# How x is turned, and the order of the first stage, in a kernel that mixes a spectral filter and a recurrence

## The chip, the core and the metric

The kernel runs on one core of one Trainium2 chip. The metric is the device time of one launch in microseconds, the median of several runs. A core has five engines that each work through a list of instructions of their own: TensorE (PE in the profile; its weight loads are PEld), VectorE (DVE), ScalarE (ACT), GpSimd (POOL) and SyncE (SP), which here only issues DMAs. They wait for each other by semaphores. DMAs are issued from a queue of SyncE, ScalarE or GpSimd and are carried out by the core's 16 DMA engines.

## The reference

The input x has 2048 tokens of 1024 features, in bfloat16. Two branches are mixed by a gate of each token.

```
g = sigmoid(sum(x * gate_w))                     # one number a token
a = irfft2(rfft2(x) * (w_r + 1j*w_i))            # over tokens and features
Bu = x @ B_bar.T                                 # B_bar complex, 1024 x 1024
h_t = Lam_bar * h_(t-1) + Bu_t                   # over the 2048 tokens
b = 2 * real(h @ C.T) + x * Dskip
out = g * a + (1 - g) * b
```

## The kernel before

**The spectral branch.** The transform over the features (called the d-transform, or fd) and the first step of the transform over the tokens (s1) work on 16 rows of tokens. Row j holds the 128 tokens whose number is j modulo 16. For a row, `fold` (VectorE, lines 661 and 662) adds and subtracts the two halves of the features, `fd(j)` (line 332) multiplies the folded row by a table G in eight matmuls and copies the result out as X1, and `s1(j)` (line 342) multiplies X1 by a table T2 in four matmuls and copies the result out as A1. A1 is stored to a scratch in DRAM (`turn_scratch`, line 353). Later stages load it in another order (`load`, line 377), take the second token step (`s2`, line 457), multiply by the weights W, and go back by two inverse token steps (`is1`, `is2`, lines 478 to 513) and the inverse d-transform (`spectral`, line 595).

**The recurrence.** `unit(c, q)` (line 253) treats chunk c of 256 tokens (eight chunks) and half q of the 1024 states. It has two halves on TensorE (line 300): 32 matmuls of B with x for the real part, 32 for the imaginary part, each followed by a copy from PSUM on ScalarE (line 302). Chunk c takes eight tokens of each of the 16 rows' two halves, so each unit reads all 16 rows of x. After its second half the unit puts seven pieces of VectorE work on a list (line 305): a rotation by a table (`turn_back`), its sums (`join`), two scans (line 275), the carry into the next chunk, a second rotation (`turn`) and its sums (`join_on`, lines 292 and 293). `early(tb)` (line 579) is the output of token tile tb (128 tokens, half of a chunk): two times 16 matmuls with C (line 570) and four with x and Dskip (line 574). It needs both units of its chunk to be done on VectorE, and it needs all of C and the tile `xs` of x. Six buffers hold units (NHA + NHB).

**How x comes.** x is loaded by eight plain DMAs of 512 KB (`load_x`, line 194) into `xn`, a place that later holds C (tiles CT). `turn_x(j)` (line 653) turns row j by eight TensorE transposes into PSUM, and ScalarE copies them into `xQ`, the turned x that everything else reads. B, C and the tiles `xs` come turned by transposing DMAs (lines 205, 555 and 562), issued by SyncE.

**What sets the order.** The order of the instructions of TensorE, VectorE and ScalarE is that of the program text (`manual_schedule`, line 169); the order on SyncE and GpSimd is chosen when the kernel is built. `front()` (line 768) does one row by a plan of letters: T for `turn_x`, f for `fold`, F for `fd(j + 1)`, S for `s1(j)`; `order` names the loads of B and C that follow a row. The halves of units and of token tiles form one chain, `ssm` (line 756), and `halves(ssm, 1)` issues the next one. From row 8 on one half follows each row. `vector(us)` (line 311) issues VectorE pieces from the list up to a given cost; `vector_until(c)` issues all that chunk c still needs. `tables` (`make_tab`, line 208) are pieces that make the rotation tables, four for each of four groups, with sines on ScalarE, casts on GpSimd and products on VectorE (lines 230 and 235). `gate()` (line 695) computes g's sum on TensorE and turns it through DRAM by two GpSimd DMAs. `load_Wcols` (line 733) loads two columns of W by ten GpSimd DMAs, called after row 3. A1 rows 0 to 7 lie in CT[0], rows 8 to 15 in a tile of four buffers.

**PSUM.** Until row 7 the unit's PSUM tile has one buffer (`psF`), the transposes have two (`psX`), and fd and s1 share two (`psA`). After row 7 `psX` and `psF` give way to `psU` with two buffers.

Of the kernel before, what the change touches and what calls it, by code (L numbers as in the profile page):

```python
# [28 lines left out]
NHA, NHB = 4, 2  # L29

# [78 lines left out]
def kernel(  # L109
# [55 lines left out]
    xctx = ExitStack()  # L165
    psF = xctx.enter_context(tc.tile_pool(name="psF", bufs=1, space=PSUM, reuse_waits="tile"))
    psX = xctx.enter_context(tc.tile_pool(name="psX", bufs=2, space=PSUM, reuse_waits="tile"))
    pools = {"u": psF}
# [18 lines left out]
    xn = [CT[i // 4][:, 2 * (i % 4):2 * (i % 4) + 2, :] for i in range(8)]  # L187
    x_v = x.rearrange("(p j) d -> p j d", j=16)
# [5 lines left out]
    def load_x(i):  # L194
        nc.sync.dma_start(out=xn[i], in_=x_v[:, 2 * i:2 * i + 2, :])
# [57 lines left out]
    def unit(c, q):  # L253
# [42 lines left out]
        for ri in range(2):  # L296
            psu = pools["u"].tile([P, 4, TC], FP32, name="psu", tag="psu")
            for j in range(4):
                for d8 in range(8):
                    nc.tensor.matmul(psu[:, j, :], lhsT=BT[4 * q + j][:, ri, d8, :],  # L300
                                     rhs=x_t[:, d8, :, :, 8 * c:8 * (c + 1)], start=(d8 == 0), stop=(d8 == 7))
            nc.scalar.copy(out=u[:, ri].rearrange("p b (q j) -> p b q j", j=32),  # L302
                           in_=psu.rearrange("p b (j q) -> p b q j", j=32))
            if ri == 1:
                work.extend([(2.4, turn_back), (1.5, join), (2.3, lambda: scan(0)), (2.3, lambda: scan(1)),
                             (0.4, carry_on), (2.4, turn), (1.4, join_on)])
            yield 3.5
# [19 lines left out]
    def gfnet():  # L327
# [4 lines left out]
        def fd(j):  # L332
            ps = psA.tile([P, 2, K], FP32, name="ps_fd", tag="ps")
            for cls in range(2):
                for d4 in range(4):
                    nc.tensor.matmul(ps[:, cls, :], lhsT=preTs[j][:, 4 * cls + d4, :], rhs=G_sb[:, cls, d4, :],  # L336
                                     start=(d4 == 0), stop=(d4 == 3))
            X1 = gta.tile([P, 2, K], BF16, name="X1")
            (nc.vector.tensor_copy if j in (3,5,7,) else nc.scalar.copy)(out=X1.rearrange("p r (i c) -> p r i c", c=2), in_=ps.rearrange("p c (r i) -> p r i c", r=2))  # L339
            X1s[j] = X1  # L340

        def s1(j):
# [7 lines left out]
            A1 = CT[0][:, j, :].rearrange("p (g k) -> p g k", g=2) if j < 8 else A1_4[:, j % 4]  # L350
            (nc.vector.tensor_copy if j < 8 else nc.scalar.copy)(out=A1, in_=psa)  # L351
            A1s[j] = A1
            nc.sync.dma_start(out=t1_w[j], in_=A1)
            if j in (8, 12):
                keep_A1(j - 4)

        def keep_A1(j):
            if j < 8:
                nc.vector.tensor_copy(out=Acol[:, :, 0:8].rearrange("p g j -> p j g"), in_=CT[0][:, :, 0:D:K])
                return  # L360
            nc.vector.tensor_copy(out=Acol[:, :, j:j + 4].rearrange("p g j -> p j g"), in_=A1_4[:, :, :, 0])

        A1s, X1s = {}, {}
        fft["fd"], fft["s1"] = fd, s1
        yield "front"
        keep_A1(12)
# [212 lines left out]
    def early(tb):  # L579
        psy = pools["u"].tile([P, D], FP32, name="ps_y", tag="psu")  # L580
# [14 lines left out]
    def spectral(tb, scale, home, eo_home=None):  # L595
        ZT_t = fft["ZT"]
        pse = pools["u"].tile([P, 4, H], FP32, name="ps_id", tag="psu")
# [55 lines left out]
    def turn_x(j):  # L653
        pt = psX.tile([P, 8, P], BF16, name="pt")
        for i in range(8):
            nc.tensor.transpose(out=pt[:, i, :], in_=xn[j // 2][:, j % 2, P * i:P * (i + 1)], identity=ident)  # L656
        nc.scalar.copy(out=xQ[:, :, j, :].rearrange("p d (g q) -> p d g q", g=2), in_=pt.rearrange("p d (q g) -> p d g q", g=2))  # L657

# [4 lines left out]

    A1_4 = gta.tile([P, 4, 2, K], BF16, name="A1", bufs=1)
    idle = A1_4[:, 3, 0]
# [9 lines left out]
    for cls in range(2):  # L675
        nc.sync.dma_start(out=fft["G"][:, cls], in_=cG[:, cls])
    load_T2(0, 2)
    load_x(1)
    load_x(2)
    load_T2(2, 8)  # L680
    for i in range(3, 8):
        load_x(i)
    load_T2(8, 16)
    assert step() == "front"
    for j in range(2):
        turn_x(j)
        fold(j)
    keep_warm(4)
    fft["fd"](0)
    rows = iter(range(2, 16))  # L690
    folds = iter(range(2, 16))
# [38 lines left out]
    nc.gpsimd.tensor_copy(out=Wp.rearrange("p r b c -> p (r b c)"), in_=xn[7][:, 0, 0:64])  # L730
    nc.gpsimd.tensor_copy(out=Wf, in_=xn[7][:, 0, 0:2])

    def load_Wcols():
        with nc.allow_non_contiguous_dma(reason="two columns of W"):
# [17 lines left out]
    def halves(gen, n):  # L752
# [3 lines left out]
    ssm = chain(unit(0, 0), unit(0, 1), unit(1, 0), unit(1, 1), unit(2, 0), early(0), unit(2, 1), early(1), unit(3, 0), early(2), unit(3, 1), early(3), unit(4, 0), early(4), unit(4, 1), early(5), unit(5, 0), early(6), unit(5, 1), early(7), unit(6, 0), unit(6, 1), early(8), early(9))  # L756

    order = {
        **{j: [(load_B, n)] for j, n in ((2, 1), (3, 1), (4, 1), (5, 2), (6, 2), (7, 2), (8, 2), (9, 2))},
        10: [(load_B, 3), (load_small,)],  # L760
        **{j: [(load_C, j - 11)] for j in range(11, 15)},
    }
    at = [0]
    tables = iter(())

    plan = {0: "FSTfTf", 1: "TSFfT", 2: "TFfTS", 3: "TFfTS", 4: "TFfTS", 5: "TFfTS", 6: "TFfTS", 7: "TFfTS"}

    def front(pieces=0):
        j = at[0]
        at[0] += 1  # L770
        for what in plan.get(j, "fFS"):
            if what == "T":
                for r in rows:
                    turn_x(r)
                    break
            elif what == "f":
                for r in folds:
                    fold(r)
                    break
            elif what == "F":  # L780
                if j + 1 < 16:
                    fft["fd"](j + 1)
            else:
                fft["s1"](j)
        for load, *args in order.get(j, ()):
            load(*args)
        for _ in range(pieces):
            next(tables, None)

    vps = psX.tile([P, 5, 8], BF16, name="vps", tag="pt")  # L790
# [67 lines left out]
    while at[0] < 16:  # L858
        j = at[0]
        front(0 if j < 4 else 1 if j < 6 else 2 if j < 10 else 3)  # L860
        if j >= 8:
            halves(ssm, 1)
        if j >= 9:
            vector(4.2)
        if j == 10:
            gate()
        if j == 15:
            for _ in tables:
                pass
            tctx.close()  # L870
        if j == 7:
            xctx.close()
            pools["u"] = ctx.enter_context(tc.tile_pool(name="psU", bufs=2, space=PSUM, reuse_waits="tile"))
        if j == 3:
            load_Wcols()
    for q in range(4, 8):
        load_C(q)
    for v, n in (("w", 4), ("a", 1), ("z", 2), ("q", 2), ("qn", 1), ("s2", 0), ("uv", 1)):
        assert step() == v
        for i in range(n):  # L880
# [6 lines left out]
            vector(3.0)  # L887
# [82 lines left out]
```

## Time and profile before

Three runs of the kernel took 340.03, 340.09 and 340.57 us. The profile is of one more execution; it gives that execution's span, from its first to its last instruction, and no other time of it.

| | |
|---|---|
| median of the runs | 340.09 us |
| span of the profiled execution | 338.3 us, 1.8 under the median |
| PE busy | 326.3 us (96%) |
| DVE busy | 292.1 us (86%) |
| ACT busy | 167.0 us (49%) |
| POOL busy | 32.1 us (10%) |
| chain of waits that ended last | PE 71%, DVE 23%, ACT 2% |
| line 656, TensorE transposes of x | 128, 9.7 us busy |
| line 657, copies of them on ScalarE | 16, 15.6 us |
| line 300, B with x | 1024, 116.6 us |
| line 336, d-transform | 119 of 128 recorded, 29.3 us |
| line 275, scans on VectorE | 32, 72.2 us |
| line 195, x by plain DMA | 8 of 512 KB, 5.8 us from issue to landing |
| line 205, B by transposing DMA | 16 of 256 KB, 5.1 us from issue to landing |

The profile has several views. The slices cut the span into 40 equal parts of 8.46 us and give each engine's busy share in tenths. The groups list instructions of one line and shape with their number, busy time and mean length. The view in order of time lists instructions with their start and length in microseconds, and where an engine was idle before one, for how long and what ended it. A matmul's length in the records is longer than the distance to the next one, since matmuls overlap; the distance from start to start is what it costs. The issue of a DMA is a row of the queue that issues it (SPq, POOLq), and its landing is later. Busy time of the DMA engines is a mean share of the 16.

### The profile page before, as it was taken

To read this page: it belongs to the slowest core of one execution; us is meant where nothing else is said; L and a number is where in the kernel's file an instruction comes from. 1 tells how busy PE (TensorE), PEld (TensorE's weight loads), DVE (VectorE), ACT (ScalarE), POOL (GpSimd) and SP (SyncE) were. 2 spreads that over 40 slices of the span, in tenths; PEclk is the share of its full clock that TensorE was granted. 3 is DMA by queue.
4 is the path that set the end of the run, shared out by engine and by line. 5 is a ranking of instruction groups with operands and counts; after the bars stand their busy time and mean duration, and the time that the engine had idled before them with its cause. 6 is when DMAs were issued, how large, how long until landed. Compare 5 with 4: busy or idle time off the path is not lost.

```text
span 338.3 us, 6201 instructions
## 1 busy us (share of the span) xinstructions
PE 326.3 (96%) x2414; PEld 212.3 (63%) x2446; DVE 292.1 (86%) x449; ACT 167.0 (49%) x211; POOL 32.1 (10%) x64
## 2 busy tenths in 40 slices
PE   8989899999999999999999999999999999999995
PEld 3445465666847575747566575869945876565552
DVE  2679948999999999999999999999980997999951
ACT  3697597836223145656557552646632243443510
POOL 1372012210000000000000000000000011121220
PEclk9999999999999999999999999999999999999999
DMA  7999999998893047889999735947203019856695
GB/s 263 409 192 212 203 217 213 163 215 205 274 213 102 2 129 180 227 202 272 259 284 260 200 135 153 224 127 215 62 2 125 32 31 147 168 109 94 110 145 166
DMA packets 83581, 58.71 MB, mean 174 GB/s; under 512 B 54328, under 2 KB 74304, under 8 KB 83424
## 3 DMA queue, kind: packets, MB, share of 16 engines
q1 hardware_dynamic: 80304, 55.64, 65.5%
q0 software_dynamic: 3168, 2.66, 8.3%
q8 instruction: 19, 0.31, 0.4%
q14 instruction: 10, 0.08, 0.1%
q10 hardware_dynamic: 80, 0.01, 0.0%
HBM read 30.49 MB, written 17.83 MB: 143 GB/s over the span
## 4 chain that ended last, share of the span: by engine, by line
PE 71%; DVE 23%; ACT 2%; issue 2%; DVEq 0%; ACTq 0%
PE ps_y L570 26%; PE psu L300 22%; PE ps_h L570 4%; DVE h L275 4%; PE ps_id L601 4%; PE ps_is L484 2%; PE ps_fd L336 2%; PE ps_is L509 2%; PE ps_is L485 2%; DVE CT L351 2%; PE ps_y L574 2%; PE ps_s L460 2%; DVE h L263 1%; DVE su L262 1%; DVE h L287 1%
## 5 line engine op out<-in xcount | busy, mean ns | idle before, releaser
L300 PE MATMUL psu<-xQ,BT 128*128 128x256 bf16 x1024 | 116.6, 273 | 0.8 <-ACT ye L588 0.5
L300 PEld LDWEIGHTS <-BT 128*128 128x128 bf16 x1024 | 98.8, 98 | 17.5 <-issue 4.5
L570 PE MATMUL ps_y<-CT,h 128*128 128x512 bf16 x436 | 99.5, 379 | 0.6
L570 PEld LDWEIGHTS <-h 128*128 128x128 bf16 x512 | 49.7, 98 | 55.2
L275 DVE TENSOR_TENSOR_SCAN h<-rz,h 128x1024 bf16<-128x1024 f32 x32 | 72.2, 2280 | 0.3
L302 ACT CAST h<-psu 128x1024 bf16<-128x1024 f32 x32 | 32.3, 1011 | 51.4 <-PE psu L300 51.3
L616 POOL DMA_DIRECT2D BT<-y_scratch x10 | 11.9, 1194 | 239.6 <-DVE BT L610 232.0
L588 ACT ACTIVATE ye<-ps_y,omg 128x512 f32<-128x512 f32 x20 | 12.7, 684 | 44.0 <-PE ps_y L574 28.7
L336 PE MATMUL ps_fd<-G_sb,preT 128*128 128x512 bf16 x119 | 29.3, 379 | 2.1 <-ACT X L339 1.0
L262 DVE TENSOR_TENSOR su<-h,tab 128x2048 bf16<-128x2048 bf16 x16 | 19.6, 1223 | 2.8 <-ACT h L302 2.2
L336 PEld LDWEIGHTS <-preT 128*128 128x128 bf16 x128 | 12.0, 97 | 15.4 <-issue 2.8
L287 DVE TENSOR_TENSOR h<-h,tab 128x2048 bf16<-128x2048 bf16 x16 | 20.7, 1295 | 0.5
L462 ACT CAST X<-ps_s 128x1024 bf16<-128x1024 f32 x16 | 16.2, 1014 | 8.7 <-PE ps_s L460 8.7
L263 DVE TENSOR_TENSOR h<-h,tab 128x2048 bf16<-128x2048 bf16 x16 | 19.6, 1225 | 0.8
L286 DVE TENSOR_TENSOR sg<-h,tab 128x2048 bf16<-128x2048 bf16 x16 | 19.5, 1220 | 0.1
L657 ACT COPY xQ<-pt 128x1024 bf16<-128x1024 bf16 x16 | 15.6, 1017 | 2.8 <-PE pt L656 2.7
L511 ACT CAST ZT<-ps_is 128x1024 bf16<-128x1024 f32 x16 | 15.5, 1024 | 2.2 <-PE ps_is L509 2.2
L339 ACT CAST X<-ps_fd 128x1024 bf16<-128x1024 f32 x13 | 13.2, 1012 | 6.2 <-PE ps_fd L336 6.1
L487 ACT CAST C<-ps_is 128x1024 bf16<-128x1024 f32 x16 | 16.1, 1007 | 0.0
L601 PE MATMUL ps_id<-raw,ZT 128*128 128x256 bf16 x128 | 15.9, 273 | 0.0
L570 PE MATMUL ps_h<-CT,h 128*128 128x512 bf16 x62 | 14.4, 379 | 0.1
L601 PEld LDWEIGHTS <-ZT 128*128 128x128 bf16 x128 | 12.4, 98 | 2.2
(186 smaller groups left out, 362.3 us busy)
## 6 DMA issues: line engine op xcount, KB each, us to landing
y_scratch<-ye SPq DMA_DIRECT2D x20, 256.0 KB, 2.6
CT<-in_A_x_dram SPq DMA_DIRECT2D x8, 512.0 KB, 5.8
Bb<-turn_scratch SPq DMA_DIRECT2D x16, 256.0 KB, 4.0
turn_scratch<-C SPq DMA_DIRECT2D x16, 256.0 KB, 3.7
raw<-turn_scratch SPq DMA_DIRECT2D x16, 256.0 KB, 4.2
Wb<-in_A_w_r_dram SPq DMA_DIRECT2D x32, 127.8 KB, 4.2
Wb<-in_A_w_i_dram SPq DMA_DIRECT2D x32, 127.8 KB, 4.1
out_dram<-BT SPq DMA_DIRECT2D x14, 256.0 KB, 2.5
```

The source lines that it names most:

```text
L262: nc.vector.tensor_mul(out=su, in0=u[:, ::-1], in1=bc(1))
L263: nc.vector.tensor_mul(out=u, in0=u, in1=bc(0))
L275: nc.vector.tensor_tensor_scan(out=seg, data0=rz[:, js].rearrange("p j t -> p (j t)"), data1=seg, initial=0.0, op0=ALU.mult, op1=ALU.add)
L286: nc.vector.tensor_mul(out=sg, in0=u[:, ::-1], in1=bc(3))
L287: nc.vector.tensor_mul(out=u, in0=u, in1=bc(2))
L300: nc.tensor.matmul(psu[:, j, :], lhsT=BT[4 * q + j][:, ri, d8, :], rhs=x_t[:, d8, :, :, 8 * c:8 * (c + 1)], start=(d8 == 0), stop=(d8 == 7))
L302: nc.scalar.copy(out=u[:, ri].rearrange("p b (q j) -> p b q j", j=32), in_=psu.rearrange("p b (j q) -> p b q j", j=32))
L336: nc.tensor.matmul(ps[:, cls, :], lhsT=preTs[j][:, 4 * cls + d4, :], rhs=G_sb[:, cls, d4, :], start=(d4 == 0), stop=(d4 == 3))
L462: nc.scalar.copy(out=X2, in_=ps2)
L487: nc.scalar.copy(out=C1.rearrange("p h (c i) -> p h c i", c=2), in_=psc.rearrange("p h (i c) -> p h c i", c=2))
L570: nc.tensor.matmul(psy, lhsT=hs[c, jb // 4][:, ri, jb % 4, P * tq:P * (tq + 1)], rhs=CT[ri][:, jb, 512 * dh:512 * (dh + 1)], start=(i == 0 ...
L601: nc.tensor.matmul(pse[:, slot, :], lhsT=ZT_t[:, i, tb, :], rhs=fft["Gi"][:, i, :], start=(kb == 0), stop=(kb == 1))
```

## The change

- `load_x(j)` brings row j by two transposing DMAs of 64 tokens each straight into `xQ`. There are 32 of them in place of the eight plain ones. `turn_x`, `xn`, `psX` and `psF` go.
- `psU` with two buffers stands from the start; fd uses it, and `psA` stays for s1 and the rest.
- A1 goes to CT[0] and CT[1]. Its copy is by VectorE in rows 6, 8, 10, 12, 14 and 15, else by ScalarE; X1's copy is always by ScalarE. The stores of A1 are issued by GpSimd.
- The loads of x, tables and the first eight parts of B are listed at the start in one order. The other eight parts of B, the small tables and all of C follow after the rows.
- All rows come before the units: the first two halves of `ssm` follow rows 14 and 15. Six units stand before the first token tile, in the order (0,0), (1,0), (0,1), (1,1), (2,0), (2,1). The gate comes after the rows, `load_Wcols` after row 12.
- Pieces of the tables and the given costs of VectorE are spread otherwise; four of the twelve warming matmuls go.

```diff
+A1_BY_VECTOR = (6, 8, 10, 12, 14, 15)
...
-    xctx = ExitStack()
-    psF = xctx.enter_context(tc.tile_pool(name="psF", bufs=1, space=PSUM, reuse_waits="tile"))
-    psX = xctx.enter_context(tc.tile_pool(name="psX", bufs=2, space=PSUM, reuse_waits="tile"))
-    pools = {"u": psF}
+    psU = ctx.enter_context(tc.tile_pool(name="psU", bufs=2, space=PSUM, reuse_waits="tile"))
...
-    xn = [CT[i // 4][:, 2 * (i % 4):2 * (i % 4) + 2, :] for i in range(8)]
-    x_v = x.rearrange("(p j) d -> p j d", j=16)
+    x_v = x.rearrange("(q g j) d -> j g q d", g=2, j=16)
...
-    def load_x(i):
-        nc.sync.dma_start(out=xn[i], in_=x_v[:, 2 * i:2 * i + 2, :])
+    def load_x(j):
+        for g in range(2):
+            nc.sync.dma_start_transpose(out=xQ[:, :, j, 64 * g:64 * (g + 1)], in_=x_v[j, g])
...
-            ps = psA.tile([P, 2, K], FP32, name="ps_fd", tag="ps")
+            ps = psU.tile([P, 2, K], FP32, name="ps_fd", tag="psu")
...
-            (nc.vector.tensor_copy if j in (3,5,7,) else nc.scalar.copy)(out=X1.rearrange("p r (i c) -> p r i c", c=2), in_=ps.rearrange("p c (r i) -> p r i c", r=2))
+            nc.scalar.copy(out=X1.rearrange("p r (i c) -> p r i c", c=2), in_=ps.rearrange("p c (r i) -> p r i c", r=2))
...
-            A1 = CT[0][:, j, :].rearrange("p (g k) -> p g k", g=2) if j < 8 else A1_4[:, j % 4]
-            (nc.vector.tensor_copy if j < 8 else nc.scalar.copy)(out=A1, in_=psa)
-            A1s[j] = A1
-            nc.sync.dma_start(out=t1_w[j], in_=A1)
+            A1 = CT[j // 8][:, j % 8, :].rearrange("p (g k) -> p g k", g=2)
+            (nc.vector.tensor_copy if j in A1_BY_VECTOR else nc.scalar.copy)(out=A1, in_=psa)
+            nc.gpsimd.dma_start(out=t1_w[j], in_=A1)
...
     load_x(0)
     for cls in range(2):
         nc.sync.dma_start(out=fft["G"][:, cls], in_=cG[:, cls])
+    load_x(1)
     load_T2(0, 2)
-    load_x(1)
     load_x(2)
     load_T2(2, 8)
-    for i in range(3, 8):
-        load_x(i)
-    load_T2(8, 16)
+    for j, b in ((3, 0), (4, 0), (5, 1), (6, 0), (7, 1), (8, 1), (9, 0), (10, 1), (11, 1), (12, 0), (13, 1), (14, 0), (15, 2)):
+        load_x(j)
+        if j == 6:
+            load_T2(8, 16)
+        load_B(b)
     assert step() == "front"
-    for j in range(2):
-        turn_x(j)
-        fold(j)
-    keep_warm(4)
+    fold(0)
     fft["fd"](0)
+    fold(1)
...
-    ssm = chain(unit(0, 0), unit(0, 1), unit(1, 0), unit(1, 1), unit(2, 0), early(0), unit(2, 1), early(1), unit(3, 0), early(2), ...
+    ssm = chain(unit(0, 0), unit(1, 0), unit(0, 1), unit(1, 1), unit(2, 0), unit(2, 1), early(0), early(1), unit(3, 0), early(2), ...
...
     def front(pieces=0):
         j = at[0]
         at[0] += 1
...
+        if j + 2 < 16:
+            fold(j + 2)
+        if j + 1 < 16:
+            fft["fd"](j + 1)
+        fft["s1"](j)
         for _ in range(pieces):
             next(tables, None)
...
     while at[0] < 16:
         j = at[0]
-        front(0 if j < 4 else 1 if j < 6 else 2 if j < 10 else 3)
-        if j >= 8:
-            halves(ssm, 1)
-        if j >= 9:
-            vector(4.2)
-        if j == 10:
-            gate()
...
+        front(0 if j < 5 else 1)
+        if j == 8:
+            fft["keep_A1"](0)
+        if j == 12:
+            load_Wcols()
+        if j >= 14:
+            halves(ssm, 1)
+            vector(2.0)
+    gate()
+    fft["keep_A1"](1)
+    load_small()
+    load_B(8)
+    for _ in range(2):
+        halves(ssm, 1)
+        for _ in range(3):
+            next(tables, None)
+        vector(3.0)
+    for _ in tables:
+        pass
+    tctx.close()
+    for q in range(8):
+        load_C(q)
+    for _ in range(4):
+        halves(ssm, 1)
+        vector(3.5)
-    for v, n in (("w", 4), ("a", 1), ("z", 2), ("q", 2), ("qn", 1), ("s2", 0), ("uv", 1)):
+    for v, n in (("w", 7), ("a", 1), ("z", 1), ("q", 1), ("qn", 1), ("s2", 0), ("uv", 1)):
...
             halves(ssm, 1)
-            vector(3.0)
+            vector(3.5)
```

## The prediction

> **What bounds the kernel now.** I read the slices of the page first, then the instructions in order of time of TensorE, VectorE and SyncE from 0 to 135 us.
>
> ```profile
> PE   8989899999999999999999999999999999999995
> DVE  2679948999999999999999999999980997999951
> DMA  7999999998893047889999735947203019856695
> ```
>
> TensorE (PE) is full from the fifth slice (8.46 us each) to the end, VectorE (DVE) from the seventh to the thirtieth, and the DMA engines from the second to the ninth. Before 40 us PE has holes. The chain of waits gives PE 71% and DVE 23%, the DVE part between 20 and 105 us. So the end is set by PE's list of matmuls plus the holes in it, and a hole comes where VectorE or a load is late. I look for such holes on both sides.
>
> ```profile
> 49.83 1.67 PE L336 MATMUL ps_fd<-G_sb,preT 128*128 128x512 bf16 x7
> 51.65 0.61 PE L348 MATMUL ps_s<-X,raw 64*128 64x512 bf16 x4
> 52.19 3.67 PE L300 MATMUL psu<-xQ,BT 128*128 128x256 bf16 x32
> 55.79 1.91 PE L699 MATMUL zps_g<-xQ,gw 128*32 128x512 bf16 x32
> ...
> 93.00 3.62 PE L570 MATMUL ps_y<-CT,h 128*128 128x512 bf16 x15
> ...
> 109.24 3.62 PE L570 MATMUL ps_y<-CT,h 128*128 128x512 bf16 x15
> ```
>
> From start to start, one d-transform (fd) takes 1.82, one s1 0.54, half a recurrence unit 3.6 in the mix and 3.5 in a row, the gate 1.84. At 93.0 the first token tile's output (e0) begins, at 109.24 the second's (e1). When e1 starts, PE has done all fd and s1, the gate, 12 halves and e0.
>
> ```profile
> 51.81 1.23 DVE L262 TENSOR_TENSOR su<-h,tab 128x2048 bf16<-128x2048 bf16 x1 [2.18 <-ACT h L302]
> ...
> 84.23 0.68 DVE L293 TENSOR_TENSOR h<-h,sg 128x1024 bf16<-128x1024 bf16 x1
> ...
> 99.54 0.69 DVE L293 TENSOR_TENSOR h<-h,sg 128x1024 bf16<-128x1024 bf16 x1
> ```
>
> VectorE starts the first unit at 51.8, ends the second at 84.9 and the third at 100.2. e0 needs units (0,0) and (0,1), the first two here: 8.1 us to spare at 93.0. Three units with what lies between them take 48.4 us.
>
> ```profile
> 24.71 5.97 SPq L205 DMA_TRANSPOSE BT<-in_B_B_im_dram  x4
> 31.35 5.99 SPq L205 DMA_TRANSPOSE BT<-in_B_B_re_dram  x4
> 38.01 3.98 SPq L205 DMA_TRANSPOSE BT<-in_B_B_im_dram  x3
> ```
>
> A transposing DMA of 128 rows (256 KB) holds SyncE's queue 1.33 us when nothing presses and 1.5 under load: 200 GB/s at best, with the DMA engines' share near 1.0. The plain x load ran at about 410 GB/s (9 to 15 us).
>
> **The change part by part.**
>
> *TensorE's transposes.* Out go 128 transposes and 4 warming matmuls, by start to start 0.43 us a row, 16 rows: 6.9 us, and about 1 us. All lie before 34 us, where PE has holes. ScalarE loses 16 copies of 1.02 (16 us) and gains 3 X1 and 2 A1 copies; VectorE loses 3 X1 (1.22) and 2 A1 (1.22): 6.1 us. All are worth something only if they bring the units earlier; that is decided by x.
>
> *x by transposing DMA.* 32 DMAs of 64 rows. No row has that shape. Bounds of its issue: half of 1.28, 0.64, if all goes by rows; 1.28 if all is per instruction. A plain DMA's issue (0.33 to 0.43) is the nearest row for the fixed part; with the rest by rows I take 0.83. Before the last x row SyncE issues 5 plain loads (0.43), 32 x, 6 B (1.33): 0.74 + 2.2 + 26.6 + 8.0 = 37.5, and 3.8 from the issue's end to the landing (median 5.1 from its start, minus 1.31): 41.3. The DMA engines give a second bound: x 4.19 MB, six B 1.57, thirteen A1 stores 3.41, at the 238 GB/s that B and stores together reached from 30 to 33 us, is 38.5; G and T2 (1.8 MB at 410) 4.5; start 2.7: 45.7. I take the middle, 43.5. Ends: 35 (0.64, quick landing) and 56 (1.28).
>
> The row decides here: 200 GB/s. [...]
>
> *The front.* PE alone: fd(0) at about 7.15 as now, then 15 fd and 14 s1: 7.15 + 15*1.82 + 14*0.54 = 42.0 for fd(15), whose fold (0.75) must start at 41.2. So even with x early the front can't pass 41.2; with x at 43.5 it is x. Every unit reads all 16 rows of x, so none can begin before. Then: fold 0.75, fd(15) 1.82, s1 0.54, half 3.6, s1 0.54, half 3.6 = 10.9; ScalarE's copy and the hand-over 1.1: VectorE's first unit starts at 43.5 + 12.0 = 55.5, against 51.8 now. PSUM doubled for fd removes 1.3 us of PE waits on X1, all inside this stretch: 0.
>
> *The new order of units.* (0,0), (1,0), (0,1), (1,1), (2,0), (2,1), then e0. PE reaches e0 at 43.5 + 10.9 + 1.84 + 35 (10 halves) + 0.4 = 91.6. But e0 now needs three units of VectorE instead of two: 48.4 from the row above; minus five folds (0.67) done before, 3.4; plus the gate's five small operations, which now stand before e0, 0.9; plus a stall: the third table's last product (L235) waits for a ScalarE scale (L229) queued behind the copy of unit (1,0)'s first half, which PE ends 5.4 us after unit (0,0): about 2.9 in all over tables three and four. Sum 48.8. So e0 starts at 55.5 + 48.8 = 104.3, and PE stands 12.7 us in front of it. Behind that wait on PE is everything else. By bounds the stall is 0, if those pieces interleave better, to 6, if a cast on GpSimd is late too.
>
> *A1 by GpSimd.* 16 stores leave SyncE (0.53 each) and cost GpSimd 1.19 each (the row of the y loads): 19 us on an engine busy 32. SyncE's 8.4 us is worth nothing where the DMA engines are full. [...] The two columns of W move from row 3 to row 12: 10 DMAs (7.1 us) and copies that wait for them, 18.6 to 29.8 now, 11 us in which GpSimd would hold stores 13 to 15, the gate's two DMAs and the casts behind it. Store 15 would land near 43.5 + 11.2 + 3 * 1.2 + 4 = 62, and the C transposes into CT[1] wait for it: 15 * 1.5 + 5 more gives 90, under the cover of e0 at 104.3 (14 us). xs(0) comes after C, and after W and MT loads (some 10 us) if SyncE keeps today's order: about 102, needed at 107.8. Both 0; if the cover goes, what is late adds one for one.
>
> *B.* Its second eight come after x on SyncE: 37.5 + 10 * 1.4 + 5 = 57, needed at 54.4 + 1.84 + 7 = 63: 0. Warming gone: 0 to 1.7, hidden by x.
>
> *Sum.* From e0 on the lists are alike: e0 7.5, then aps and zps 0.7, and e1 starts at 112.5 with the same work done that PE has at 109.24. Later waits don't move: before, VectorE is 11 to 31 us ahead of every later token tile. So +3.3 on the span of 338.3: 341.6. The median of the runs (340.09) is 1.8 over the span: 343.4.
>
> **Rivals.**
>
> *Faster: x keeps PE's pace.* For it: 3.3 to 3.5 us landings of lone transposes, ScalarE freed of 16 us. Then fold(15) at 41.2, no stall of the tables: first unit 53.2, e0 at 53.2 + 45.9 = 99.1, e1 at 107.3: -1.9, 338.2. Against it: the DMA share near 1.0 in the trace. It decides from a last x row before about 42 and stalls under 1.5.
>
> *Even.* x in time but with the stall: e1 at 110.2, 341.0; or late by 1 without it, 339.2. Its middle is no change.
>
> *Much slower: the issue of a transposing DMA is per instruction.* At 1.28 for 64 rows, x15 lands at 0.74 + 2.2 + 41 + 8 + 3.8 = 55.7, 12.2 after my value: 355.6. It decides from 0.9 a DMA upward.
>
> *The change doesn't do what it says:* the recurrence still can't run ahead of B and x, and the freed PE time only becomes waiting; that is the forecast itself.
>
> **How the numbers follow.** Forecast (0.8 to 7 slower): 0.53, 343.4. Faster: 0.22, 338.2. Even: 0.10. Much slower: 0.15, 350 to 358. About 0.2% (0.7 us) is what a measurement of this kernel can tell from no change. Faster 0.22, same 0.10, slower 0.53 + 0.15 = 0.68. The range takes in the forecast's ends, most of the faster case and the lower part of the last: 337.5 to 353.
>
> **What would show it.** In the changed trace: x transposes on SyncE back to back from 0.7 to 37 or later, about 0.83 each; the last landing near 43.5; folds waiting for DMA; VectorE's first unit near 55.5; PE idle some 12 us before the first ps_y, released by L293's join; GpSimd in line with 1.2 us stores. It is wrong if PE doesn't wait before e0, if the last x row lands before 41, or if a load (C, xs) is what e0 waits for.

## The result and the profile after

The changed kernel takes 364.39 us (median of 4 runs, 363.67 to 365.46) against 340.33 for the kernel before in the same session: a ratio of 1.0706, interval [1.0685, 1.0726]. It is slower, as forecast, but by 24 us instead of 3, outside the range. The profiled execution took 363.67 us, its span is 361.9, and the mean granted clock of TensorE is 0.965. Of the kernel f1 below, one execution in four, the profiled one, fell in a slower state, and it is told by the other three.

First the slices of the page, 9.05 us each.

```profile
PE   5969756999995399999999999999999999999996
DVE  1554634639999969999999999999995399999961
...
PEclk9998995999999589999999999999999999999999
DMA  6699679999998823079998996297612107976595
```

Behind the third slice TensorE now has two dips: slices 5 to 7 (36 to 63 us), and slices 13 and 14 (109 to 127 us). VectorE is full only from the tenth slice (81 us); before, from the eighth of 8.46 us (59 us). The granted clock falls to 5 tenths in both dips (slices 7 and 14). In the six slices in which x is issued the DMA engines stand at 0.6 to 0.7 four times and at 0.9 twice: for most of that time they are not what x waits for.

The row of x's transposing DMAs, by source line (nanoseconds of one issue as minimum, median and maximum; then first and last start):

```profile
L193 SPq DMA_TRANSPOSE xQ<-in_A_x_dram x32: 1199/1270/1707, 0.7 to 53.3; - x32
...
  DVE preT L647: 25.7, 10
  POOL Wp L715: 20.8, 1
...
DMA to landing us min/median/max: 2.7/3.5/5.8
```

A DMA of 64 rows holds SyncE's queue 1.27 us at the median, as long as B's of 128 rows in the kernel before (1.28 us at least, 1.31 the median of its imaginary half). The last starts at 53.3, so with the median landing row 15 is there near 56.8. This is an estimate: no instruction waited for row 15, and the last parts of rows 13 and 14 took 5.4 and 5.1 us, so it may have been up to 2 us later. Who waited: VectorE's folds, ten times, 25.7 us; and GpSimd, once, 20.8 us. That second wait returns on ScalarE. GpSimd and then ScalarE, in order of time:

```profile
45.71 0.52 POOL L715 COPY Wp<-xQ 128x64 bf16<-128x64 bf16 x1 [20.76 <-DMA xQ<-in_A_x_dram]
...
54.50 0.60 POOL L725 DMA_DIRECT2D Wf<-in_A_w_i_dram  x1
...
55.89 0.78 POOL L218 CAST tab<-sn_f 128x512 bf16<-128x512 f32 x1
```

```profile
56.70 0.63 ACT L784 ACTIVATE sn_f<-ang 128x512 f32<-128x512 f32 x1 [9.82 <-POOL tab L218]
57.23 0.99 ACT L337 CAST X<-ps_fd 128x1024 bf16<-128x1024 f32 x1
```

The copy that prepares W's columns reads row 12 of x. Behind it on GpSimd stand ten DMA issues and then the cast of a table (L218); ScalarE's next sine needs that cast's tile, and behind the sine stands the copy X1 of row 12, whose matmuls TensorE had ended at 49.24. Then VectorE and TensorE:

```profile
75.40 1.23 DVE L260 TENSOR_TENSOR su<-h,tab 128x2048 bf16<-128x2048 bf16 x1 [3.48 <-ACT h L300]
...
123.37 0.69 DVE L291 TENSOR_TENSOR h<-h,sg 128x1024 bf16<-128x1024 bf16 x1
```

```profile
58.28 1.04 PE L346 MATMUL ps_s<-X,raw 64*128 64x512 bf16 x4 [2.98 <-ACT X L337]
59.25 3.59 PE L334 MATMUL ps_fd<-G_sb,preT 128*128 128x512 bf16 x8
...
111.37 1.89 PE L562 MATMUL ps_y<-CT,h 128*128 128x512 bf16 x7
123.51 3.77 PE L562 MATMUL ps_y<-CT,h 128*128 128x512 bf16 x8 [10.25 <-DVE h L290]
127.50 4.18 PE L562 MATMUL ps_y<-CT,h 128*128 128x512 bf16 x16
131.73 3.62 PE L562 MATMUL ps_y<-CT,h 128*128 128x512 bf16 x15
```

VectorE's first unit starts at 75.40 (51.81 before) and its third ends at 124.06 (100.23 before). TensorE stands 10.25 us before e0 for exactly that, and e1 starts at 131.73 (109.24 before). After it TensorE waits at most 0.53 us at a time; before, too. So all but 1.1 us of the loss is there by 132 us.

**The account that holds.** The sums of busy time from 0 to the end of VectorE's third unit, before and after:

```profile
sum 100.20, PE 94.31 PEld 58.58 DVE 82.25 ACT 63.54 POOL 20.20; mean PE 47.15 PEld 29.29 DVE 41.12 ACT 31.77 POOL 10.10
```

```profile
sum 124.06, PE 95.66 PEld 55.02 DVE 78.83 ACT 55.46 POOL 34.70; mean PE 47.83 PEld 27.51 DVE 39.41 ACT 27.73 POOL 17.35
```

VectorE's work up to there is 3.4 us less; its idle time is 100.20 - 82.25 = 18.0 us before and 124.06 - 78.83 = 45.2 after. 27.2 - 3.4 = 23.8, and the spans differ by 23.6. The whole question is therefore why VectorE stands idle 27 us longer in the front.

### The profile page after: what moved, and what is told of

Same layout as the page of the kernel before. It is cut to its first block, busy times and chain, and to the rows that moved or that the text cites. A ratio compares the mean times of both kernels' runs of the same rounds, so it can differ in the third digit from the quotient of the medians.

```text
span 361.9 us, 5965 instructions
## 1 busy us (share of the span) xinstructions
PE 328.1 (91%) x2289; PEld 205.5 (57%) x2314; DVE 288.0 (80%) x443; ACT 157.0 (43%) x200; POOL 46.7 (13%) x80
## 4 chain that ended last, share of the span: by engine, by line
PE 68%; DVE 12%; SPq 10%; DMA 3%; POOL 2%; issue 2%; ACT 2%; DVEq 0%; ACTq 0%; POOLq 0%
PE ps_y L562 27%; PE psu L298 22%; SPq L193 8%; PE ps_h L562 4%; DVE h L273 4%; PE ps_id L593 3%; PE ps_is L476 2%; PE ps_is L501 2%; PE ps_is L477 2%; PE ps_y L566 2%; SPq L203 2%; PE ps_s L452 2%; DMA G_sb<-c_G 1%; DMA Wf<-in_A_w_i_dram 1%; DVE h L285 1%
## 5 line engine op out<-in xcount | busy, mean ns | idle before, releaser
L298 PE MATMUL psu<-xQ,BT 128*128 128x256 bf16 x1024 | 115.2, 273 | 0.8 <-ACT ye L580 0.5
L562 PE MATMUL ps_y<-CT,h 128*128 128x512 bf16 x432 | 102.1, 385 | 11.0 <-DVE h L290 10.2
L334 PE MATMUL ps_fd<-G_sb,preT 128*128 128x512 bf16 x125 | 36.0, 434 | 13.4 <-DVE preT L647 9.9
L608 POOL DMA_DIRECT2D BT<-y_scratch x10 | 12.0, 1200 | 246.7 <-DVE BT L602 237.6
L580 ACT ACTIVATE ye<-ps_y,omg 128x512 f32<-128x512 f32 x20 | 12.7, 684 | 48.0 <-PE ps_y L566 43.5
L647 DVE TENSOR_TENSOR preT<-xQ 128x512 bf16<-128x512 bf16 x16 | 6.9, 431 | 26.0 <-DMA xQ<-in_A_x_dram 25.7
L337 ACT CAST X<-ps_fd 128x1024 bf16<-128x1024 f32 x16 | 16.1, 1007 | 17.9 <-PE ps_fd L334 17.9
L261 DVE TENSOR_TENSOR h<-h,tab 128x2048 bf16<-128x2048 bf16 x16 | 19.6, 1225 | 0.8
L285 DVE TENSOR_TENSOR h<-h,tab 128x2048 bf16<-128x2048 bf16 x16 | 19.6, 1225 | 0.5
L346 PE MATMUL ps_s<-X,raw 64*128 64x512 bf16 x64 | 10.7, 416 | 3.5 <-ACT X L337 3.5
```

The source lines that it names most:

```text
L261: nc.vector.tensor_mul(out=u, in0=u, in1=bc(0))
L285: nc.vector.tensor_mul(out=u, in0=u, in1=bc(2))
L562: nc.tensor.matmul(psy, lhsT=hs[c, jb // 4][:, ri, jb % 4, P * tq:P * (tq + 1)], rhs=CT[ri][:, jb, 512 * dh:512 * (dh + 1)], start=(i == 0 ...
```

## The experiments

The table holds every kernel: time (median), ratio to the kernel before with its interval, and from the profiled execution the start of VectorE's first unit, the end T of its third, and the span less T.

| kernel | us | ratio | first unit | T | span - T |
|---|---|---|---|---|---|
| before | 340.3 | 1 | 51.8 | 100.2 | 238.1 |
| after | 364.4 | 1.0706 [1.0685, 1.0726] | 75.4 | 124.1 | 237.8 |
| e1_x128 | 357.4 | 1.0489 [1.0365, 1.0613] | 71.9 | 120.5 | 236.8 |
| e2_wcols_row3 | 360.0 | 1.0565 [1.0401, 1.0728] | 73.5 | 122.9 | 237.6 |
| e3_both | 352.7 | 1.0351 [1.0321, 1.0381] | 64.6 | 113.2 | 237.6 |
| e4_stores_sp | 364.9 | 1.0709 [1.0678, 1.0740] | 76.4 | 125.7 | 237.3 |
| e5_x128_wlate | 357.4 | 1.0493 [1.0355, 1.0630] | 70.9 | 119.5 | 237.5 |
| e6_x_tensor | 353.9 | 1.0389 [1.0280, 1.0499] | 65.9 | 114.6 | 237.0 |
| e7_before_order | 340.5 | 1.0002 [0.9966, 1.0039] | 51.6 | 101.4 | 238.3 |
| e8_before_gpstore | 341.9 | 1.0049 [1.0029, 1.0069] | 51.8 | 100.8 | 239.7 |
| f1_casts_vec | 360.7 | 1.0589 [1.0538, 1.0639] | - | - | - |
| f2_x128_casts | 351.6 | 1.0331 [1.0294, 1.0367] | 63.5 | 112.2 | 238.3 |
| f3_old_order | 364.1 | 1.0706 [1.0671, 1.0741] | 78.9 | 127.6 | 236.1 |
| f4_x128_casts_order | 351.6 | 1.0356 [1.0281, 1.0431] | 62.2 | 112.7 | 236.0 |
| g1_x_free | 350.6 | 1.0294 [1.0270, 1.0317] | 63.2 | 111.9 | 236.7 |
| g2_x_free_casts | 351.4 | 1.0313 [1.0280, 1.0347] | 62.5 | 111.2 | 238.1 |
| g3_b_after_x | 364.4 | 1.0720 [1.0663, 1.0778] | 79.8 | 128.5 | 237.9 |
| g4_x128_b_after_x | 351.0 | 1.0304 [1.0279, 1.0329] | 62.8 | 111.5 | 238.0 |
| h1_x_free_units | 356.3 | 1.0434 [1.0396, 1.0473] | 51.4 | 105.6 | 250.0 |
| h2_x128_units | 352.3 | 1.0318 [1.0286, 1.0351] | 59.3 | 110.8 | 239.7 |

(Of f1 only times are read.) Read the last column first: it is 236 to 240 in all but h1. What comes behind VectorE's third unit is the same everywhere; T decides.

### One part of the change at a time

**e7: the kernel before with only the new order of units.**

```
-    ssm = chain(unit(0, 0), unit(0, 1), unit(1, 0), unit(1, 1), unit(2, 0), early(0), unit(2, 1), early(1),
+    ssm = chain(unit(0, 0), unit(1, 0), unit(0, 1), unit(1, 1), unit(2, 0), unit(2, 1), early(0), early(1),
```

> The kernel before with the new order of units alone: (0,0), (1,0), (0,1), (1,1), (2,0), (2,1), then the first token tile. Theory (the token tile now needs three units of VectorE; before, VectorE ends the third at 100.2 and TensorE would come to the tile at 100.0): a wait of 0 to 2 us, time 340 to 342. Rival (the order by itself costs the 10 us that TensorE waits in the changed kernel): 348 to 351.

340.48: as expected, no cost. TensorE and VectorE were in step in the kernel before: with the third unit ending at 101.4, TensorE arrives no earlier and does not wait for it.

**f3: the changed kernel with the old order** (the same two lines, turned round).

> The changed kernel with the order of units of before: the first token tile's output after (0,0), (0,1), (1,0), (1,1), (2,0). It then needs two units of VectorE, not three: they end at 110.8 in the changed kernel's trace where the third ends at 124.1, PE gets there near 104, and the second tile's output starts near 126.4 instead of 131.7: 358 to 360. Rival: the order is free here as it was in the kernel before (+0.14 us there), because VectorE's list behind it sets the end anyway: 363.5 to 365.5.

364.11, the rival. e1 does start 3.7 us earlier (128.00), but TensorE then waits for VectorE at other places, the last of them behind e1:

```profile
109.74 1.67 PE L562 MATMUL ps_y<-CT,h 128*128 128x512 bf16 x6 [1.48 <-DVE sg L284]
113.54 3.73 PE L562 MATMUL ps_y<-CT,h 128*128 128x512 bf16 x8 [2.13 <-DVE h L290]
...
147.76 0.25 PE L443 MATMUL qps<-Qb,Sel_sb 128*128 128x16 bf16 x4 [3.04 <-DVE Qb L438]
```

So "three units instead of two before e0", over which the prediction took such care, is not the cause: VectorE's whole list is late, and the order mainly decides where TensorE meets it. It is not quite free in this trace: the profiled execution had its first unit 3.5 us later than the changed kernel's (row 14 was folded at 59.82 instead of 55.78), and behind T it was 1.7 us shorter (236.1 against 237.8). So the old order is worth some 2 us here, where the expectation had 5.

**e8: the kernel before with A1 stored by GpSimd.**

```
-            nc.sync.dma_start(out=t1_w[j], in_=A1)
+            nc.gpsimd.dma_start(out=t1_w[j], in_=A1)
```

> The kernel before with A1 stored by GpSimd alone. Theory (SyncE's 8 us of store issues are not what sets the time there, GpSimd has room): 339 to 341.5. Rival (GpSimd's hold on casts and on A1's buffers costs as it does in the changed kernel): 344 to 350.

341.87, 1.6 us more [1.0, 2.3 by the interval]: small, slightly above the expectation. **e4: the changed kernel with the same line turned back.**

> As the changed kernel, but A1 is stored by SyncE again. Theory (SyncE's queue is the bound until the last x row): some 13 stores of 0.53 us stand before it, the units begin 5 to 7 us later, time 369 to 372, unless the builder puts the stores behind x, where it is 363 to 365. Rival (the stores on GpSimd are what costs): 355 to 361.

364.85: the second case named there. The stores went behind x and the first eight parts of B on SyncE (first at 57.66), and neither helped nor hurt.

**e6: the changed kernel with x turned by TensorE again.** Eight plain loads, 128 transposes, sixteen copies by ScalarE; the first eight parts of B follow x, all else as changed.

```
-            nc.sync.dma_start_transpose(out=xQ[:, :, j, 64 * g:64 * (g + 1)], in_=x_v[j, g])
+        nc.sync.dma_start(out=xn[i], in_=x_v[:, 2 * i:2 * i + 2, :])
...
+            nc.tensor.transpose(out=pt[:, i, :], in_=xn[j // 2][:, j % 2, P * i:P * (i + 1)], identity=ident)
+        nc.scalar.copy(out=xQ[:, :, j, :]..., in_=pt...)
```

> The changed kernel with its x route alone undone: eight plain DMAs, eight TensorE transposes a row in PSUM slots shared with s1, copies on ScalarE; the first eight parts of B follow x; all else (rows first, six units before the first token tile, A1 by GpSimd, W's columns after row 12) as changed. Theory (the x route is the loss, the order costs little more than the wait before the first token tile): TensorE paces the rows at 2.8 us, the units begin at 49 to 53, VectorE's first unit starts at 57 to 61, the wait before the first token tile stays at about 10 us, time 345 to 350. Rival (the order and GpSimd's part are the loss): 356 to 364.

353.91, between theory and rival. 10.5 of the 24 us go with x's route and B's place behind it; 13.6 stay, with ScalarE busy 20.00 of the 20 us from 30 to 50.

### x's issue and GpSimd's hold

**e1: x in 16 DMAs of 128 tokens.**

```
-        for g in range(2):
-            nc.sync.dma_start_transpose(out=xQ[:, :, j, 64 * g:64 * (g + 1)], in_=x_v[j, g])
+        nc.sync.dma_start_transpose(out=xQ[:, :, j, :], in_=x_v[j])
```

> x comes by 16 transposing DMAs of 128 tokens in place of 32 of 64; the tokens of a row of 128 then lie in another order, so the output isn't the reference's. Theory (an issue of a transposing DMA costs SyncE 1.3 us whatever its rows, and that queue sets when the units begin): the last x issue ends near 54.6 - 16 * 1.3 = 34, the units on TensorE begin between 46 and 52 instead of 66.5, and the time is 345 to 350. Rival (the bytes through the DMA engines set it): each DMA of 128 rows holds the queue twice as long, the units begin at 64 to 67, and the time is 362 to 366.

357.37, between theory and rival. The source row of x in this kernel:

```profile
L192 SPq DMA_TRANSPOSE xQ<-in_A_x_dram x16: 1231/1364/3987, 0.7 to 39.4; - x16
```

Twice the rows, and nearly the same issue (1.23 us at least, 1.36 at the median; 1.20 and 1.27 at 64 rows): between these two shapes an instruction costs about the same. x is issued 14 us earlier, by 40.7. That is not the 34 expected. Now the DMA engines press (0.9 or more in every slice of its page from the second to the twelfth; a mean share of 0.94 in the first 20 us, 0.67 in the changed kernel), and single x issues took up to 3.99 us, those of B 2.2 and 2.8 at the median (1.3 and 1.4 in the changed kernel), and the last row landed 8.5 us after its issue began, near 47.9. The first unit comes only 3.5 us earlier: GpSimd's hold stands there alone now (fold(14) at 45.6, fold(15) at 58.6).

**e2: W's columns after row 3, with copies that read row 2.** **e3: e1 and e2 together.**

```
-        if j == 12:
+        if j == 3:
             load_Wcols()
...
-        nc.gpsimd.tensor_copy(out=Wp..., in_=xQ[:, 0, 12, 0:64])
+        nc.gpsimd.tensor_copy(out=Wp..., in_=xQ[:, 0, 2, 0:64])
```

> As the changed kernel, but the two columns of W are loaded after row 3, and the copies ahead of them read row 2 of x and not row 12. Theory (GpSimd stands before row 12's x and then in ten DMA issues, a sine on ScalarE waits 9.8 us for a cast behind them, and this delays the last rows by some 6 us): the units begin at 60 to 61 instead of 66.5, time 357.5 to 359.5. Rival (only x's landing counts, the wait of ScalarE lies beside it): 363 to 365.

> 128-token x DMAs and W's columns after row 3 together; the order of tokens in a row is changed, so the output isn't the reference's. Theory (both in one chain, TensorE sets the pace of the rows when both are gone): the units begin at 43 to 47, the first token tile still waits for VectorE's third unit, time 339 to 344. Rival (DMA engines full, or another wait in the rows): over 350.

e2: 359.95, near the expectation; its two runs (357.6, 362.3) leave the interval wide. ScalarE's wait is gone, but W's ten small DMAs (7.5 KB at most) now run beside x, whose last issue ends at 58.26 instead of 54.64. e3: 352.68, the rival's size: x is issued by 48.9 there, not 41, and the first unit is at 64.6.

**e5: e1 with the call for W's columns behind the tables.**

```
-        if j == 12:
-            load_Wcols()
...
     tctx.close()
+    load_Wcols()
```

> 128-token x DMAs as in the first experiment (other order of tokens in a row, so the output isn't the reference's), and W's columns are loaded after the tables, so that neither GpSimd's hold nor their small packets lie in the rows. Theory (two things make the loss of the rows: SyncE's 1.3 us an issue, and GpSimd; without both, x comes as fast as the DMA engines carry it, which the prediction put at a last row near 43.5): last x issue ends at 39 to 41, VectorE's first unit starts at 54 to 57, time 342 to 347. Rival (the 350.8 us span of the run with both is already all that can be had, something else delays the units): 350 to 353.

357.42: both missed, because the edit did not do what it says. GpSimd still had the copy for W, with 12.95 us of waiting, ahead of the last tables' casts: on GpSimd the order is chosen when the kernel is built, and is not that of the text.

**f1: the tables' two casts on VectorE. f2: the same with 128-token DMAs.**

```
-        nc.gpsimd.tensor_copy(out=tab[:, 1, js, :], in_=sn_f)
+        nc.vector.tensor_copy(out=tab[:, 1, js, :], in_=sn_f)
...
-        nc.gpsimd.tensor_copy(out=tab[:, 0, js, :], in_=cs_f)
+        nc.vector.tensor_copy(out=tab[:, 0, js, :], in_=cs_f)
```

> The changed kernel with the tables' two casts to bf16 on VectorE instead of GpSimd, so that nothing ScalarE needs stands behind GpSimd's copies and DMAs of W's columns; x still comes in 64-token DMAs. If that hold is what delays VectorE's first unit from x15 + 12 (69.2) to 75.4 us, the first unit starts near 69 to 70 and the time falls by 6.2 less about 1 for the casts that now stand in VectorE's list: 358 to 360. Rival: ScalarE's late sine is the last of several waits that end together (x itself, ScalarE's own list), and VectorE only takes work on: 363.5 to 366.

> Both terms that the forecast had wrong put right at once: x in 16 DMAs of 128 tokens (token order within a row changed, so the output is in another order of tokens) and the casts on VectorE. If the issue of x and the hold are the whole miss, the last x row lands near 44.5, VectorE's first unit starts near 56.5 and the time is 342 to 346, the forecast plus about 1. Rival: the transposing stream is held back by the DMA engines as soon as issue is not the limit (the last issue was at 48.9 when W's columns ran beside it), and the first unit comes at 62 to 65: 349 to 353.

f1: 360.65 (358.46 to 361.60), a little over the theory; the ratio falls from 1.0706 to 1.0589, 4 us. Net of the casts that VectorE now has, the hold is worth about 4, not 5.2, and the three times lie 3 us apart. f2: 351.55, the rival's size but not its reason. x is issued by 40.7 and the last two folds do not wait for it, yet the first unit comes at 63.5. **f4: f2 with the old order** (f3's lines).

> All three together: 128-token DMAs (tokens in another order), casts on VectorE, old order of units. If the three are independent, 5 less than the run with the first two: 337 to 341, which is the kernel before. Rival: with the first unit early enough PE is the limit and the order is worth nothing: the same as the run with the first two.

351.57, the same as f2: the order changes nothing that can be told from this run's spread (349.74 to 354.57).

### With x taken out

**g1: x by plain loads as if it were turned already; the first eight parts of B follow x. g2: the same with f1's edit.**

```
-            nc.sync.dma_start_transpose(out=xQ[:, :, j, 64 * g:64 * (g + 1)], in_=x_v[j, g])
+        nc.sync.dma_start(out=xQ[:, :, 2 * i:2 * i + 2, :].rearrange("p d j q -> p d (j q)"), in_=x_v[i])
```

> The changed kernel with x loaded by 8 plain DMAs as if it lay turned in memory already (nothing turns it, so the output is not the reference's): x costs neither issue time nor TensorE. If x is what is late, the front runs at TensorE's own pace and this is the forecast's case of x early: 338 to 342. Rival: the front's own lists (TensorE, ScalarE and VectorE handing each row on) need 2.8 to 3 us a row whatever x does: units from 53 to 55, first unit of VectorE at 60 to 63, 346 to 350.

> The same with the tables' casts on VectorE. If GpSimd's copies of W's columns still hold the tables when x is early, 3 to 6 less than g1; if the hold came only from the late row 12, the same as g1 within 1.5.

350.64 and 351.40: the rival of g1, and no hold left (g2 is not faster). This is the decisive pair. With x for nothing, 10 of the 24 us remain; so x's route explains 13.8 (with the hold, which comes from the late row 12), and the prediction's "x keeps PE's pace" could not have given 338. TensorE in g1, in order of time:

```profile
7.92 3.17 PE L333 MATMUL ps_fd<-G_sb,preT 128*128 128x512 bf16 x8 [3.10 <-DMA G_sb<-c_G]
...
13.88 1.90 PE L333 MATMUL ps_fd<-G_sb,preT 128*128 128x512 bf16 x8
...
25.02 3.19 PE L333 MATMUL ps_fd<-G_sb,preT 128*128 128x512 bf16 x8 [3.97 <-DVE preT L646]
28.14 0.96 PE L345 MATMUL ps_s<-X,raw 64*128 64x512 bf16 x4
29.03 1.90 PE L333 MATMUL ps_fd<-G_sb,preT 128*128 128x512 bf16 x8
...
51.89 1.90 PE L333 MATMUL ps_fd<-G_sb,preT 128*128 128x512 bf16 x8
```

fd(15) starts at 51.89, where the prediction had 42.0 "by PE alone". The 9.9 us: fd(2) at 13.88 instead of 7.15 + 2 * 1.82 + 0.54 = 11.33 (G arrives late, TensorE waits 3.10 for it, and fd(0) takes 3.17 instead of 1.90, with a granted clock of 0.84 from 5 to 10 us and 0.82 from 10 to 15): 2.6. A hole of 3.97 at 21 us: the folds stand on VectorE behind the tables' constants, and those behind ScalarE's sine, as VectorE shows:

```profile
19.48 0.17 DVE L796 TENSOR_TENSOR sTC<-s2c,r_sb 128x8 f32<-128x8 f32 x1 [2.91 <-ACT s2c L782]
21.50 0.17 DVE L797 TENSOR_TENSOR cTC<-c2c,r_sb 128x8 f32<-128x8 f32 x1 [1.85 <-ACT c2c L784]
...
24.55 0.42 DVE L646 TENSOR_TENSOR preT<-xQ 128x512 bf16<-128x512 bf16 x1
```

The low clock after that hole (0.66 from 25 to 30 us): fd 3.19 and s1 0.96 instead of 1.90 and 0.60: 1.7. Waits for folds later: 0.51 and 0.74, and some 0.4 of smaller gaps. And VectorE's sum in g1, to 111.4, half a microsecond before the end of its third unit:

```profile
sum 111.40, PE 91.53 PEld 54.17 DVE 77.89 ACT 55.24 POOL 33.61; mean PE 45.76 PEld 27.09 DVE 38.94 ACT 27.62 POOL 16.81
```

33.5 us idle, 15.6 more than before, though x costs almost nothing. The largest group of it is not x but VectorE's own copies of A1, which wait for TensorE (11.2 us; 1.0 in the kernel before):

```profile
L348 DVE CAST CT<-ps_s 128x1024 bf16<-128x1024 f32 x6 | 7.3, 1223 | 11.2 <-PE ps_s L345 11.2
L646 DVE TENSOR_TENSOR preT<-xQ 128x512 bf16<-128x512 bf16 x16 | 6.9, 434 | 3.9 <-DMA xQ<-in_A_x_dram 3.9
```

A row gives VectorE 0.7 to 1.9 us of work (folds, and in six rows A1's copy) and takes TensorE 2.37. Before, units ran between the last rows and filled VectorE; now all 16 rows come first.

**g3 and g4: B's first eight transposes behind x**, with 64-token and with 128-token DMAs (and f1's edit).

```
         load_x(j)
...
-        load_B(b)
+    load_B(8)
```

> The changed kernel with 64-token DMAs, the casts on VectorE, and the first eight transposes of B behind x in SyncE's queue instead of between its rows. The last x issue then ends some 7 x 1.33 earlier, near 45.5, and x15 is there near 49; B's first four follow by 51 and land near 55, so units start at 55 to 57 and VectorE's first unit at 64 to 66: 350 to 353. Rival: the first units now wait for B instead, or the front's lists are the limit: 356 to 361.

> The same with 128-token DMAs (tokens in another order): x is issued by about 27 us and landed by 32. If x was still late in f2, this gains on it and comes near g2; if the front's lists are the limit, it is f2 again: 349 to 352.

g3: 364.40, worse than both. Row 15 is folded at 52.20, 11 us earlier than in the changed kernel, and then the first unit waits for B:

```profile
61.83 1.05 PE L298 MATMUL psu<-xQ,BT 128*128 128x256 bf16 x8 [1.22 <-DMA BT<-in_B_B_im_dram]
73.47 5.26 PE L298 MATMUL psu<-xQ,BT 128*128 128x256 bf16 x24 [10.59 <-DMA BT<-in_B_B_im_dram]
```

The 10.59 us are not the sum of 40 issues, which at 1.3 us each would have been over near 57. SyncE's queue shows the last four parts of B (before them, the first four took 6.00):

```profile
52.94 19.92 SPq L203 DMA_TRANSPOSE BT<-in_B_B_im_dram  x4
```

That is 4.98 us for one, against 1.50 in the four before them. From 51.57 to 58.1 GpSimd issued nine stores of A1 in a row, which had stood behind W's columns. That they are what holds the queue is not shown: f2 has the same pair (eight stores from 52.76, four parts of B in 15.10 us from 53.83), but the changed kernel has four parts in 11.70 from 67.19 without such a row of stores. So 1.27 us, the median of x's issues in the changed kernel, is near the least that one took (1.20), and not what one always takes. g4: 351.04, f2 and g1 again: with x early the rows' own lists are the limit.

**h1: g1 with units from row 8 on, between the rows, as before. h2: f2 with units from row 11 on.**

```
-        front(0 if j < 5 else 1)
+        front(0 if j < 4 else 1 if j < 6 else 2 if j < 10 else 3)
...
-        if j >= 14:
+        if j >= 8:
             halves(ssm, 1)
-            vector(2.0)
+        if j >= 9:
+            vector(4.2)
```

In both, B's second eight are issued ahead of the rows' loop and fewer halves follow behind it; h2 has 11 and 12 in place of 8 and 9, and the pieces as in f2.

> g1 (x loaded plainly as if already turned, output not the reference's) with recurrence units issued from row 8 on between the d-transforms, and the tables' pieces at the pace of before, instead of all 16 rows first. If the remaining 10 us come from 16 rows standing ahead of the first unit, VectorE's first unit is back at 50 to 54 us and the time at 338 to 342, that of the kernel before. Rival: VectorE and ScalarE have the same folds, copies and tables to do either way, so what is gained at the first unit is lost between the units, and the time stays at 347 to 351.

> f2 (x in 128-token DMAs, tokens in another order; casts on VectorE) with units issued from row 11 on and the second eight of B right behind x. x15 is there near 44.5, so the first half can run near 46 and the second near 51: first unit of VectorE at 55 to 58 against 63.5, time 343 to 347. Rival as for h1: no change, 350 to 353.

h1: 356.25, slower than g1, outside both. The first unit is back at 51.4 and the third ends at 105.6, 6.3 earlier than in g1. So the order of rows and units, with the tables' pieces at their old pace, is worth 6.3 of g1's 11.7 us at that point. But behind T it loses more than that. TensorE comes to e0 only at 108.32, and then waits for loads. In h1 the last store of A1 is issued at 91.14 (72.41 in the changed kernel), the transposes of C into the same place begin at 96.81, and the second `xs` comes behind W's loads on SyncE, at 122.47 (111.39 in the changed kernel):

```profile
126.67 0.61 PE L565 MATMUL ps_y<-dgD,xs 128*128 128x128 bf16 x4 [6.11 <-DMA xs<-in_A_x_dram]
```

h2: 352.32, no gain, the rival. The third unit ends 1.4 earlier than in f2, and span - T is 1.4 longer. The nearest that a kernel with the changed front comes to the kernel before is 351, in g1 (which leaves x's turning out), g2, g4, f2 and f4.

## Why the prediction failed, step by step

In spans: 361.9 measured, 341.6 forecast, 20.3 short.

- **"x by transposing DMA", the step that failed.** The prediction took 0.83 us for an issue of 64 rows, between ends 0.64 and 1.28, and x15 at 43.5. It is 1.27, the upper end: last start 53.3, landing 3.5 later, x15 at 56.8, 13.3 more. Its rival "per instruction" had this mechanism and 55.7, and with 355.6 us was still 8.8 short, mostly for the next item. The upper end had a row (1.28 at 128 rows); the fixed part was taken from plain DMAs, another kind of operation. e1 shows it by halving the instructions. The second bound, 45.7 by the DMA engines, was nearly right for e1, which has x15 near 47.9. And the "1.5 under load" was too little. The kernel before has three in a row that took 2.65 each, beside x's plain loads:

```profile
13.41 7.96 SPq L205 DMA_TRANSPOSE BT<-in_B_B_re_dram  x3
```

- **"A1 by GpSimd. Both 0".** The hold was named, with its 11 us of W's issues and the casts behind it, but only the stores were followed on to their readers; that ScalarE's sine waits for a cast, and X1 of a row behind the sine, was left to a bound. From x15 to the first unit it took 75.4 - 56.8 = 18.6 us instead of 12.0: 6.6 more. About 4 of it is the hold (f1), which may take in some of the 1.7 of the low clock in fd(14) (0.50 from 59.2 to 63 us), 3.59 instead of 1.90. If x15 came up to 2 us later than 56.8, as much belongs to the item above. The store's issue was priced at 1.19 and took 0.72, which changed nothing.
- **"The front: 41.2 by PE alone"** was wrong by 10 as well (g1: fold(15) at 51.41), hidden here by the later x. So the case "x early" at 338.2 was not to be had; with x in time the kernel still takes 351.
- **First unit to e0: 48.8** forecast, 123.51 - 75.40 = 48.1 measured, and for the reason given: the stall before a product of the third table, priced at 2.9 with the fourth, shows as one wait of 2.35 (L233). **e0 to e1: 8.2** forecast, 8.2 measured, by luck: eight of e0's matmuls ran before the wait, the 0.7 of aps and zps came behind e1's start, and the low clock after the wait (0.50 from 123.5 to 127.5 us, 0.87 from there to 131.7) made up for both. **TensorE before e0: 12.7** forecast; 10.25, after part of e0 had run at 111.37. **Behind e1** 1.1 more than forecast.
- **"The new order"** was priced at the whole 12.7 us of waiting. e7 shows it free, f3 and f4 within 2 us: the mechanism (VectorE's list is what TensorE waits for) was right, the order as its cause wrong.
- **SyncE's stores and "B later: 0"**: e4 and e8 agree on the first within 1.6 us. For B's second eight it held: in the changed kernel the units' matmuls stand idle 0.8 us in all. The first eight are another matter: in g3, behind x, they are late by 10.59.

Sum: 13.3 + 6.6 - 0.7 + 0 + 1.1 = 20.3.

By issue time x's transposing DMAs carried 128 KB per 1.27 us, 103 GB/s, where the prediction's row had 200 at 128 rows; e1, with 128 rows, has 256 KB per 1.36 us (its median), 193.

The other 5.4 us of g1's lateness at T can be read in h1's trace, though no run takes them out. There VectorE stands idle 27.2 us up to T (18.0 before): its A1 copies wait 6.3 (1.0 before), the first small vectors 4.5 (1.0), which follow fd(0) on TensorE, and the tables' constants 5.0 for ScalarE's sines (none before). Its work is 3.9 us less. Of h1's 12 us behind T, 6.11 + 0.95 are waits for loads; for the rest, TensorE comes to e0 2.8 us after T, where in the changed kernel eight of e0's matmuls had run before it. What stays open is what each of these is worth by itself, and what holds the queue in g3. The hold and the late x were not separated without a side effect on W's DMAs or VectorE's list.

## What to carry to other kernels

When a step moves to a DMA, price it per instruction on the issuing queue with the same kind of DMA, and take the upper end where no row has the shape; keep what the DMA engines carry as a second bound. Then find the engine whose list ends last, and count its idle time up to the joint where others wait for it: here 18 us before, 45 after, and the difference, less 3.4 us of work, is the result. Ahead of an in-order queue that is made to wait (here GpSimd's, 20.8 us), follow every instruction behind it to its reader, not only the ones that were moved.

## What the hardware showed unexpectedly

- A transposing DMA costs nearly the same issue time at 64 rows (1.20 us at least, 1.27 median) as at 128 (1.23 and 1.36). Beside other transfers single ones of 128 rows held the queue up to 3.99 (e1) and 5.66 us (B in the changed kernel), and four in a row 19.92 (g3).
- A DMA issue on GpSimd for a 256 KB store took 0.72 us (L350's `DMA_DIRECT2D`), less than the 1.19 of the accumulating loads.
- After a wait of 3.97 us in g1 the granted clock is 0.66 from 25 to 30 us, and eight matmuls took 3.19 us instead of 1.90. After 10.25 us in the changed kernel it is 0.50 from 123.5 to 127.5 us and 0.87 from there to 131.7, and the sixteen matmuls of the second stretch took 4.18 instead of 3.62. After shorter waits there matmuls were slow too: fd(13) took 2.72 us after a wait of 2.81 (0.68 from 52.5 to 55.4 us), and fd(14) 3.59 after one of 2.98 before it (0.50 from 59.2 to 63). No run here settles why.
